# Batch 0 of a windowed attention feeding a gated two-matmul layer: scores four blocks wide, values read where they land, whole copies, weights loaded in smaller pieces, a new table of biases

## The chip, the cores and the metric

One core of one Trainium2 chip runs the kernel. The metric is the device time in microseconds (us) of one execution; the kernel before takes 299.81 us (median of 3 runs, 299.52 to 299.89). Engines are named as the profile names them: PE is TensorE (its weight loads are PEld), DVE is VectorE, ACT is ScalarE, POOL is GpSimd, SP is the sync engine, which only issues transfers.

## The reference

Attention over 8 batches, 8 heads, 576 rows and a head width of 64, followed by a layer with a sigmoid gate over all 4608 rows:

```python
scores = scale * np.matmul(q, k.transpose(0, 1, 3, 2))
rel = pos[:, None] - pos[None, :]
mask_plain = (rel >= 0) & (rel < 32)
mask_dil = (rel >= 0) & (rel < 32 * 4) & (rel % 4 == 0)
# heads 0-3 use mask_plain, heads 4-7 mask_dil; softmax over the unmasked scores
attn_out = np.matmul(attn, v)
x = attn_out.transpose(0, 2, 1, 3).reshape(4608, 512)
h = x @ w_in                      # 512 -> 2048
g = h * (1.0 / (1.0 + np.exp(-beta * h)))
out = g @ w_out                   # 2048 -> 512
```

So a row sees at most 32 keys: the 32 before it in the plain heads, every fourth of 128 in the dilated ones. Nearly all of the arithmetic is in the two matrix products.

## The kernel before, in words

**The layer.** The rows are cut into nine tiles of 512. For each tile t, `slot_h` runs 16 times (fb, 128 of the 2048 columns each): four matmuls of 512 columns (L901) of `w_in_bf` with `xT`, the transposed attention output; a tanh on ACT (L910); the gate on DVE (L915), which writes `g`. `block` runs four times per tile (128 rows each): 16 matmuls (L936) in four parts, each part with four fb of `w_out_bf` and needing only the quarter of w_out that it reads; then the result leaves PSUM through ACT or DVE (L951, L953) and is stored by SP. The first four fb of tile 0 are "apart": they first multiply the dilated half of x (kt 2, 3) and only then the plain half, in two pieces of rows.

**The attention**, `attention(b, ...)`, goes through a batch with named steps. x = 0, 1 are the two pairs of plain heads, x = 2, 3 the two pairs of dilated heads. In batches 0 to 2 q and k come from DRAM as rows (cast to bf16 on the way) and are transposed on PE (KD, QD for the dilated heads, L483; KP, QP for the plain ones, L493) and copied out of PSUM. S steps are scores. The plain rows are cut into six blocks of 96 queries per pair of heads; a plain score step of batches 0 and 1 takes three blocks (j = 0 or 1) of one x for both heads into two PSUM banks (L761), from batch 3 on all blocks go at once, four to a bank (L725). In batch 0 a mask is added in PSUM before the scores, as a matmul of the identity with a band of 0 and -65536 (L687, L747, L750); later batches multiply by a mask after the exponential (L637). The exponential is on ACT (L633). V steps are the products with v (L802 dilated, L818 plain): v carries a 65th column of ones, so that the last column is the softmax sum; DVE then takes its reciprocal and scales (L652, L653). X steps transpose the result back on PE (L855, L870) and copy it into `xT` (L862 and L878, through the helper at L257). T, U and Y do the same for the last 16 dilated positions of each residue.

The dilated v lands in `vd16` without the column of ones; the step `spread` (L619 to L625) copies it into `vd`, which has that column, in every batch. The dilated output of one x is copied into `xT` in two halves of time (L859): 288 and 224 columns.

**The order of the work** is worked out when the program is built. Each step is an operation in class `Plan` with the engines it can run on, an assumed cost, its dependencies and a due value `vt`. The plan picks, again and again, the operation that can start first by its model, and among those that start about equally early on an engine the one with the smallest `vt`. `NUDGE` adds a bias of so many ns to the start of the operation with a given number before the comparison (76 of about 1300 operations have one; the numbers count the operations as they are made, so that any operation added or left out shifts those behind it). `CAPS` says how many PSUM banks, of eight, each kind of step may hold at once: "o" is for output blocks, 3 of them. Each engine then executes its own list strictly in that order. Where PE would have nothing to do before 80 us the plan inserts a filler, a matmul on zeros (L1057, L1059). At most eight transfers per issuing engine are outstanding; the next issue waits for the oldest.

**Loads.** POOL issues the casting loads. In order of due value: batch 0's q, k and v (-9 to -8.4); w_in in three pieces of 512, 512 and 1024 columns (-7.3 to -7.28, L967); batch 1's q and k rows (-7.25 to -7.22) with w_out's first half between them (-7.235), batch 1's dilated v (-7.20), w_out's second half (-7.19, L972), batch 1's plain v (-7.19). POOL also builds the masks, as operations of its own: the tail mask (due -7.295), `mask_d` (-7.215) and `mask_n` (-7.183).

## Time and profile before

| | before |
|---|---|
| time, median of 3 runs (lowest, highest) | 299.81 us (299.52, 299.89) |
| the profiled execution: span, first to last instruction | 298.3 us |
| mean granted TensorE clock | 0.999 |
| first h matmul (L901) | 18.44 us |
| first output matmul (L936) | 34.81 us |
| first h matmul of tile 1 | 52.09 us |
| last PE work ends | 295.2 us |
| DMA, mean over the span | 141 GB/s |

The profile shows one execution. Its span is 298.3 us; the time of a run also holds what lies before the first and after the last instruction, and the median of the runs is 1.5 us above that span. A timeline row gives the start, the length, the engine and line, the operation with output and inputs, how many instructions are merged, and in brackets how long the engine idled before it and what ended that. PE's matmuls are pipelined: the length of a row includes the last one's latency, so rows overlap. A group row gives the busy time of the group, the mean ns of one instruction, and the idle time before them with its releasers. A row of the chain has a start, a length and what worked. Sizes of loads are those at the destination, in bf16.

### The profile page before, as it was taken

What the parts mean: (1) busy time and instruction counts of PE and PEld (TensorE: products, weight loads), DVE (VectorE), ACT (ScalarE), POOL (GpSimd) and SP (SyncE); (2) the same over time, 40 slices, a digit from 0 to 9 for tenths busy, and PEclk for the clock granted to TensorE, in tenths of its full rate; (3) what the DMA queues carried; (4) which work ended last, traced back from release to release, by engine and by line L of the source; (5) the groups of instructions that cost most, each with busy time, mean ns of one, the idle gap of its engine ahead of it and who ended that gap; (6) DMA issues with size and microseconds to landing.
All of it is one profiled execution on the core that took longest, in us unless ns stands there. A gap on an engine that the chain in (4) does not pass through costs nothing.

```text
span 298.3 us, 6224 instructions
## 1 busy us (share of the span) xinstructions
PE 293.0 (98%) x2424; PEld 149.8 (50%) x2424; DVE 186.1 (62%) x422; ACT 169.8 (57%) x308; POOL 90.4 (30%) x126
## 2 busy tenths in 40 slices
PE   8999999999999999999999999999999999999995
PEld 6765456545554445444544454445444444444454
DVE  4879668888767658774589358936891075433300
ACT  3768876867456738642487348634862376445311
POOL 8987354654283026600551065000100000000000
PEclk9999999999999999999999999999999999999999
DMA  7999999999979995999999989995115200010122
GB/s 150 187 208 202 206 196 210 154 163 184 185 124 226 151 199 124 171 136 240 184 188 155 200 174 196 162 186 147 38 31 124 73 0 36 35 37 37 63 76 73
DMA packets 111249, 42.00 MB, mean 141 GB/s; under 512 B 87620, under 2 KB 104596, under 8 KB 111220
## 3 DMA queue, kind: packets, MB, share of 16 engines
q0 software_dynamic: 60336, 18.58, 59.6%
q1 hardware_dynamic: 50740, 22.95, 36.4%
q8 instruction: 19, 0.31, 0.4%
q10 hardware_dynamic: 144, 0.07, 0.1%
q14 instruction: 10, 0.08, 0.1%
HBM read 37.76 MB, written 18.87 MB: 190 GB/s over the span
## 4 chain that ended last, share of the span: by engine, by line
PE 86%; DMA 8%; POOL 2%; DVE 1%; issue 1%; ACT 0%; POOLq 0%
PE bank L936 42%; PE bank L901 36%; DMA w_out_bf<-in_moe_w_out_dram 6%; DMA w_in_bf<-in_moe_w_in_dram 2%; PE bank L818 2%; PE bank L697 1%; PE bank L802 1%; PE bank L725 1%; POOL vp L408 1%; PE bank L787 1%; PE bank L666 0%; PE bank L761 0%; POOL st L408 0%; DVE g L915 0%; PE bank L493 0%
## 5 line engine op out<-in xcount | busy, mean ns | idle before, releaser
L936 PE MATMUL bank<-w_out_bf,g 128*128 128x512 bf16 (+2 forms) x608 | 136.6, 368 | 0.4 <-DMA w_out_bf<-in_moe_w_out_dram 0.4
L901 PE MATMUL bank<-xT,w_in_bf 128*128 128x512 bf16 (+2 forms) x584 | 134.8, 376 | 0.1
L915 DVE SCALAR_TENSOR_TENSOR g<-tnh,bank 128x512 bf16<-128x512 bf16 x144 | 96.5, 683 | 51.5 <-ACT tnh L910 50.3
L910 ACT ACTIVATE tnh<-bank,beta_half 128x512 bf16<-128x512 f32 x144 | 98.4, 690 | 53.2 <-PE bank L901 47.4
L901 PEld LDWEIGHTS <-w_in_bf 128*128 128x128 bf16 x584 | 55.1, 98 | 60.6 <-issue 0.2
L936 PEld LDWEIGHTS <-g 128*128 128x128 bf16 x608 | 55.2, 98 | 57.8 <-DMA w_out_bf<-in_moe_w_out_dram 0.5
L951 ACT ACTIVATE osb<-bank 128x512 f32<-128x512 f32 (+1 forms) x30 | 17.6, 592 | 34.1 <-PE bank L936 29.5
L633 ACT ACTIVATE ptd<-bank 128x512 bf16<-128x512 f32 x32 | 17.0, 600 | 21.4 <-PE bank L697 21.4
L633 ACT ACTIVATE pt<-bank 128x384 bf16<-128x384 f32 (+1 forms) x54 | 21.1, 463 | 6.5 <-PE bank L725 4.1
L637 DVE TENSOR_TENSOR pt<-pt,mask_n 128x384 bf16<-128x384 bf16 (+1 forms) x39 | 14.5, 378 | 12.1 <-ACT pt L633 11.6
L653 DVE TENSOR_TENSOR xsp<-bank,rcp 96x384 bf16<-96x384 f32 x32 | 17.7, 554 | 1.1
L637 DVE TENSOR_TENSOR ptd<-ptd,mask_d 128x512 bf16<-128x512 bf16 x25 | 10.9, 448 | 11.3 <-ACT ptd L633 10.4
L953 DVE TENSOR_SCALAR osb<-bank 128x512 f32<-128x512 f32 (+2 forms) x8 | 4.9, 607 | 20.5 <-PE bank L936 20.5
L652 DVE RECIPROCAL rcp<-bank 128x4 f32<-128x4 f32 (+2 forms) x72 | 12.8, 177 | 3.5 <-PE bank L818 1.4
L408 POOL DMA_DIRECT2D vt<-in_v_dram x16 | 13.7, 864 | 4.0 <-DMA w_out_bf<-in_moe_w_out_dram 2.9
L637 POOL TENSOR_TENSOR pt<-pt,mask_n 128x288 bf16<-128x288 bf16 (+1 forms) x7 | 5.3, 764 | 31.2 <-ACT pt L633 31.2
L653 DVE TENSOR_TENSOR xdm<-bank,rcp 128x256 bf16<-128x256 f32 x32 | 13.6, 424 | 1.1
L408 POOL DMA_DIRECT2D s<-in_k_dram x10 | 12.9, 1286 | 0.6 <-issue 0.6
L1015 POOL COPY pace<-xT 1x2 bf16<-1x2 bf16 x4 | 0.7, 176 | 39.2 <-DMA xT<-x 39.2
L408 POOL DMA_DIRECT2D s<-in_q_dram x10 | 12.2, 1220 | 0.1
L818 PEld LDWEIGHTS <-pt 128*128 128x128 bf16 x192 | 8.9, 97 | 4.4
L408 POOL DMA_DIRECT2D vp<-in_v_dram x9 | 10.2, 1129 | 1.0 <-DVE g L915 0.8
(113 smaller groups left out, 186.8 us busy)
## 6 DMA issues: line engine op xcount, KB each, us to landing
out_dram<-osb SPq DMA_DIRECT2D x35, 256.0 KB, 3.8
s<-in_q_dram POOLq DMA_DIRECT2D x10, 288.0 KB, 10.2
s<-in_k_dram POOLq DMA_DIRECT2D x10, 288.0 KB, 9.0
w_out_bf<-in_moe_w_out_dram POOLq DMA_DIRECT2D x2, 1024.0 KB, 17.4
vp<-in_v_dram POOLq DMA_DIRECT2D x7, 288.0 KB, 13.5
st<-in_q_dram POOLq DMA_DIRECT2D x6, 288.0 KB, 10.0
x<-xsp SPq DMA_DIRECT2D x12, 144.0 KB
st<-in_k_dram POOLq DMA_DIRECT2D x5, 288.0 KB, 13.2
```

The source lines that it names most:

```text
L408: {"POOL": nc.gpsimd, "SP": nc.sync}[queue].dma_start(out=out, in_=in_)
L633: nc.scalar.activation(out=w(), in_=sc(), func=ACT.Exp, scale=SCALE)
L637: E[e].tensor_tensor(out=w(), in0=w(), in1=m(), op=ALU.mult)
L652: nc.vector.reciprocal(out=r, in_=p[..., D])
L653: nc.vector.tensor_tensor(out=dst, in0=p[..., 0:D], in1=r.unsqueeze(len(p.shape) - 1).to_broadcast(list(p.shape[:-1]) + [D]), op=ALU.mult)
L818: nc.tensor.matmul(pv[:, a, h2, :], lhsT=lhs, rhs=vp[kv][:, (2 * x + h2) * NI + 3 * j + a, 0:D + 1], start=True, stop=True)
L901: nc.tensor.matmul(bank(g)[:, a:z], lhsT=w_in_bf[:, kt, fb * P:(fb + 1) * P], rhs=xT[:, kt, xo + a:xo + z], start=(i == 0 and kt == kts[0] ...
L910: nc.scalar.activation(out=th[:, 0:n], in_=bank(g)[:, 0:n], func=ACT.Tanh, scale=beta_half[:, fb:fb + 1])
L915: nc.vector.scalar_tensor_tensor(out=g_t[t % 2][:, fb, c0:c0 + n], in0=th[:, 0:n], scalar=1.0, in1=bank(g)[:, 0:n], op0=ALU.add, op1=ALU.mult)
L936: nc.tensor.matmul(bank(g)[:, lo:hi], lhsT=g_t[t % 2][:, fb, tb * P:(tb + 1) * P], rhs=w_out_bf[:, fb, lo:hi], start=(fb == 0), stop=(fb = ...
L951: nc.scalar.mul(out=ob[:, lo:hi], in_=bank(g)[:, lo:hi], mul=0.5)
L953: nc.vector.tensor_single_scalar(out=ob[:, lo:hi], in_=bank(g)[:, lo:hi], scalar=0.5, op=ALU.mult)
```

## The change

All of it but the biases and the bank count touches batch 0 and the loads of the weights.

- **Plain scores, batch 0** (`FOURS`): three steps of four blocks in the place of four steps of three blocks. The twelve blocks of the two x run through, so that the second step holds blocks 4, 5 of x = 0 and 0, 1 of x = 1. Six exponentials of 384 columns stand in the place of eight of 288, and the values of x, j wait for the steps that hold their blocks. The mask matmuls and their columns stay. The dependencies at batch 1 are extended, since batch 0 now lays its blocks out otherwise in the same buffer.
- **Dilated values, batch 0** (`LANDED`): no `spread`. The product reads `vd16` directly, 64 columns wide, and a second matmul of one column, with the ones of `vd[0]`, gives the sum: 16 matmuls more. The reader recorded for `vd16` is then the value step and not the copy.
- **Dilated copies, batch 0** (`WHOLE`): one copy of 512 columns per x into `xT` in the place of two.
- **Weights**: w_in in five pieces (256, 256, 512, 512, 512 columns; due -7.30 to -7.26), w_out in four (due -7.257, -7.256, -7.182, -7.181), each part of an output block waiting for its own quarter.
- **Order**: `CAPS["o"]` 4; `NUDGE` is a new table of some 760 entries between -2500 and 2500 ns.

```diff
-    CAPS = {"h": 4, "p": 4, "o": 3, "z": 4, "a": 8, "s": 5, "w": 6}
+    CAPS = {"h": 4, "p": 4, "o": 4, "z": 4, "a": 8, "s": 5, "w": 6}
-    NUDGE = {6: 2500, 32: -2500, 44: 150, 45: -400, 58: -150, 72: 60, 76: -400, 88: -400, 96: 60,
...
+    NUDGE = {0: -150, 1: -60, 2: -2500, 3: -900, 4: -150, 5: -60, 6: 150, 7: -60, 8: -60, 9: -60,
...
+    LANDED = 1
+    WHOLE = 1
+    FOURS = 1
...
-        o = plan.op([("POOL", 1100), ("DVE", 620), ("ACT", 1030)], spread,
-                    [ld["vd"][0], (fill3, fill4)[kv]] + war(("vd", kv)), vt, sbuf=True)
...
+        if b >= LANDED:
+            o = plan.op([("POOL", 1100), ("DVE", 620), ("ACT", 1030)], spread, ...
+            vdeps["D"] = [o]
+        else:
+            vdeps["D"] = [ld["vd"][0], fill3]
...
+            if b < FOURS:
+                if x and j:
+                    continue
+                m = 2 * j + x
+                blocks = range(4 * m, 4 * m + 4)
...
+                before = plan.op([("PE", 2 * mm(4 * QT) + 50)], added, [ident, adds["P"]], vt, acquire=gs)
+                sop = plan.op([("PE", 4 * mm(QT))], score,
+                              [o for y in sorted({n // NI for n in blocks}) for o in steps[f"KP{y}"] + steps[f"QP{y}"]] + [before],
+                              vt, group=gs, halves=True)
...
+                            src, n = (vd[kv], D + 1) if b >= LANDED else (vd16, D)
+                            nc.tensor.matmul(pv[:, r, a, 0:n], lhsT=ptd[:, x - 2, j, 2 * r + a],
+                                             rhs=src[:, 2 * (x - 2) + a, 2 * r + j, 0:n],
                                              start=True, stop=True)
+                            if b < LANDED:
+                                nc.tensor.matmul(pv[:, r, a, D:D + 1], lhsT=ptd[:, x - 2, j, 2 * r + a],
+                                                 rhs=vd[0][:, 0, 0, D:D + 1], start=True, stop=True)
...
-                for j, (t0, t1) in enumerate(((0, CT // 2), (CT // 2, P))):
+                for j, (t0, t1) in enumerate(((0, P),) if b < WHOLE else ((0, CT // 2), (CT // 2, P))):
...
-    for n, (c0, c1) in enumerate(((0, 512), (512, 1024), (1024, 2048))):
+    for n, (c0, c1) in enumerate(((0, 256), (256, 512), (512, 1024), (1024, 1536), (1536, 2048))):
...
-    for n in range(2):
-        o = load("POOL", (w_out_bf[:, 8 * n:8 * n + 8, :],
-                          moe_w_out[n * 8 * P:(n + 1) * 8 * P, :].rearrange("(c p) d -> p c d", p=P)),
-                 [], (-7.235, -7.19)[n], 2048, .41)
-        w_out_ld[2 * n] = w_out_ld[2 * n + 1] = o
+    for n in range(4):
+        w_out_ld[n] = load("POOL", (w_out_bf[:, 4 * n:4 * n + 4, :],
+                                    moe_w_out[n * 4 * P:(n + 1) * 4 * P, :].rearrange("(c p) d -> p c d", p=P)),
+                           [], (-7.257, -7.256, -7.182, -7.181)[n], 1024, .41)
```

## The prediction

> **What bounds the kernel now.** I read the page's busy table first.

> ```profile
> PE 293.0 (98%) x2424; PEld 149.8 (50%) x2424; DVE 186.1 (62%) x422; ACT 169.8 (57%) x308; POOL 90.4 (30%) x126
> ```

> TensorE (PE) is busy for 293.0 of 298.3 us, so the only time to be had is time in which it does nothing of use. The windows, cut at the first h matmul, the first w_out matmul and the first matmul of tile 1, show where that is (columns: window, its length, busy us of PE, PEld, DVE, ACT and POOL with instruction counts, granted clock, DMA share, GB/s).

> ```profile
> 10.00:18.44 8.44, 8.11 (x193) 6.17 (x188) 7.90 (x23) 6.08 (x17) 7.33 (x12) 1.00 1.52 193
> 18.44:34.81 16.37, 15.98 (x128) 8.73 (x119) 12.42 (x26) 13.53 (x23) 10.57 (x18) 1.00 1.24 206
> 34.81:52.09 17.28, 17.28 (x245) 9.51 (x246) 12.38 (x34) 12.38 (x31) 8.84 (x11) 1.00 1.53 203
> 100.00:200.00 100.00, 99.89 (x708) 48.49 (x708) 69.01 (x154) 56.26 (x100) 30.66 (x35) 1.00 1.38 178
> ```

> From 18.44 on PE idles 0.39 us up to 34.81, nothing in the next window and 0.11 in the hundred that stand for the middle. Before 18.44 its busy time deceives: the PE timeline (start, length, what, count, idle before it) shows fillers, matmuls on zeros that the plan puts wherever PE would wait.

> ```profile
> 11.22 0.71 PE L1059 MATMUL bank<-zero 128*128 128x256 bf16 x5
> 12.10 0.39 PE L1059 MATMUL bank<-zero 128*128 128x256 bf16 x2
> 12.57 0.41 PE L802 MATMUL bank<-vd,ptd 128*128 128x65 bf16 x8
> 12.82 0.38 PE L1059 MATMUL bank<-zero 128*128 128x256 bf16 x2
> 15.52 0.82 PE L1059 MATMUL bank<-zero 128*128 128x256 bf16 x6
> 17.22 0.38 PE L1059 MATMUL bank<-zero 128*128 128x256 bf16 x2
> 18.03 0.48 PE L493 MATMUL bank<-ident_b,st 64*64 64x64 bf16 x36 [0.25 <-DMA st<-in_q_dram]
> 18.44 1.04 PE L901 MATMUL bank<-xT,w_in_bf 128*128 128x512 bf16 x4
> 34.81 1.04 PE L936 MATMUL bank<-w_out_bf,g 128*128 128x512 bf16 x4 [0.39 <-DMA w_out_bf<-in_moe_w_out_dram]
> ```

> Six fillers take 0.82 us and two 0.38, so one more costs 0.44 / 4 = 0.11 us. From 11.22 to 18.44 there are 5+2+2+6+2 = 17, or 1.9 us. With the waits of 0.25 and 0.39 that makes 2.5 us; this is all the front has to give after 11 us. The engine that holds PE up there is VectorE: 7.90 busy of 8.44.

> **Values where they land, whole copies, wider scores.** The DVE timeline of batch 0:

> ```profile
> 11.26 0.75 DVE L257 COPY qT<-bank 128x576 bf16<-128x576 bf16 x1
> 12.03 0.43 DVE L257 COPY vd<-vd 128x1024 bf16<-128x1024 bf16 x1
> 12.69 0.42 DVE L257 COPY vp<-vp 32x640 bf16<-32x640 bf16 x1 [0.23 <-DMA vp<-in_v_dram]
> 13.04 0.16 DVE L652 RECIPROCAL rcp<-bank 128x4 f32<-128x4 f32 x1
> 17.02 0.76 DVE L257 COPY xT<-bank 128x288 bf16<-128x288 bf16 x2
> 19.08 0.28 DVE L637 TENSOR_TENSOR ptt<-ptt,mask_t 96x256 bf16<-96x256 bf16 x1
> 33.08 0.84 DVE L637 TENSOR_TENSOR ptd<-ptd,mask_d 128x512 bf16<-128x512 bf16 x2
> ```

> The removed spread is the vd copy at 12.03. The first dilated values (12.57) come right behind it, and the first norm at 13.04 behind those. Without it the values wait for the load and for their exponentials:

> ```profile
> 5.33 1.00 POOL L408 DMA_DIRECT2D vd<-in_v_dram  x1
> vd<-in_v_dram POOLq DMA_DIRECT2D x1, 256.0 KB, 6.4
> 9.48 1.57 ACT L633 ACTIVATE ptd<-bank 128x512 bf16<-128x512 f32 x3
> ```

> The load lands at 5.33 + 6.4 = 11.7 (the last column of such a row is us from issue to landing), and three of the four exponentials end by 9.48 + 1.57 = 11.05. So the values can run at 11.8 and the norm can start at 11.8 + 0.4 = 12.2, once DVE has finished qT at 12.01. That is up to 0.8 earlier. Each group now also issues a one-column matmul beside each of its four, 16 in all. PE runs eight 65-column ones in 0.24 us further on, 0.03 each:

> ```profile
> 44.63 0.24 PE bank L802 x8
> 40.91 0.23 PE bank L761 x6
> 41.15 0.97 PE bank L936 x4
> 42.90 1.73 PE bank L936 x8
> ```

> So the sixteen cost at most 0.48 us of PE and more than nothing, because they are issued one by one. I take the upper end, the same kind of matmul; what hides them is the 1.9 us of fillers, and if those were gone the 0.48 would be paid. On the chain, eight of them stand ahead of the first norm at worst: 0.2 us. I take 0.6 for the spread, with ends 0 (DVE then only waits for something else, the halo of vp at 12.69 being the next late thing) and 0.8. [...]

> The whole dilated copy replaces 288 + 224 columns by 512. By groups, ScalarE takes 403 and 359 ns for the two, and VectorE 403 and 380:

> ```profile
> L257 ACT COPY xT<-bank 128x288 bf16<-128x288 bf16 x9 | 3.5, 403 | 1.1 <-PE bank L870 1.0
> L257 ACT COPY xT<-bank 128x224 bf16<-128x224 bf16 x3 | 1.1, 359 | 0.0
> L633 ACT ACTIVATE pt<-bank 128x384 bf16<-128x384 f32 x30 | 12.6, 501 | 4.1 <-PE bank L725 4.1
> L633 ACT ACTIVATE pt<-bank 128x288 bf16<-128x288 f32 x24 | 8.5, 415 | 2.4 <-PE bank L761 2.2
> ```

> A slope of 44 ns per 64 columns puts the whole one at 403 + 154 = 557 on ACT, 0.2 less than two, but if two engines would have shared the halves it is 0.15 later than the longer of them. Before, X3's two copies ran one behind the other on DVE (17.02, 0.76), and the first h matmul waits for them, so I take a gain of 0.1 (from -0.15 to +0.2). Six exponentials of 384 instead of eight of 288 are 6 x 501 = 3.0 against 8 x 415 = 3.3 us of ACT. ACT has 2.4 us free in that window, so I take 0 (0 to 0.3). Mask matmuls and scores keep their columns, 8 x 288 = 6 x 384 = 2304, and cost nothing new. The values of x = 1 now wait for the third score group, but their output is read last: the four "apart" groups start on the dilated rows, 8 matmuls at 1.73 / 8 = 0.22, 1.7 us of cover. Without it that wait is late next.

> **The first h matmul.** At 18.03 PE stands 0.25 us in front of the second batch's q transposes, which are not needed yet. With loads and biases reordered I expect those behind the first h: they are moved, not saved, so only the 0.25 counts (0 if another wait takes the place).

> **Weights.** Loads from POOL land in the order issued:

> ```profile
> 9.58 6.91 DMA w_in_bf<-in_moe_w_in_dram
> 16.78 0.91 POOL L408 DMA_DIRECT2D w_out_bf<-in_moe_w_out_dram  x1 [0.44 <-DMA w_in_bf<-in_moe_w_in_dram]
> 12.20 1.51 POOL L408 DMA_DIRECT2D w_in_bf<-in_moe_w_in_dram  x2
> w_in_bf<-in_moe_w_in_dram POOLq DMA_DIRECT2D x1, 512.0 KB, 8.3
> w_in_bf<-in_moe_w_in_dram POOLq DMA_DIRECT2D x1, 1024.0 KB, 12.5
> 25.71 0.90 POOL L408 DMA_DIRECT2D w_out_bf<-in_moe_w_out_dram  x1 [0.66 <-DMA w_in_bf<-in_moe_w_in_dram]
> w_out_bf<-in_moe_w_out_dram POOLq DMA_DIRECT2D x1, 1024.0 KB, 16.7
> st<-in_q_dram POOLq DMA_DIRECT2D x1, 288.0 KB, 6.5
> ```

> w_in's three pieces land at 9.58 + 6.91 = 16.5, 12.20 + 8.3 = 20.5 and about 12.95 + 12.5 = 25.4 (the two issues at 12.20 share 1.51), w_out's halves at about 34.8, when PE's wait ends, and 25.71 + 16.7 = 42.4. So the 1024 KB of the third piece took 4.9 us, 209 KB per us. Of w_out's first half the first quarter is enough to begin: behind the same bytes it lands 512 / 209 = 2.4 us before 34.8, at 32.3, and ahead of the second rows earlier still. The wait of 0.39 goes; with h begun about 1 us sooner PE gets there at 33.4, and the quarter is there. w_in's first piece, halved, lands 256 / 209 = 1.2 sooner, at 15.3, ahead of any h I expect. Two issues are added for each matrix, at 0.75 to 0.9 us of POOL each, 3.4 in all. Behind them on POOL stand the tail mask, first read at 19.08, and the masks of batch 1, first read at 33.08; all were built by 25, so the second have 8 us of cover. The tail mask has less, and its reader delays only batch 0's tail rows, which the first h tile doesn't read. The issue at 16.78 stood behind the landing of an earlier one, so smaller pieces free it sooner, too.

> What a cut costs in the queue the rows bound: between 16.5 and 20.5 landed the second rows' q of 288 KB and w_in's second piece of 512, 800 KB in two loads in 4.0 us, where 209 KB per us makes 3.83. So a further load costs at most 0.17 us and perhaps nothing; w_in's two would put w_out's first quarter at 32.6, still ahead of PE. [...]

> **A fourth o bank and new biases.** The critical rows above show the price of going from 64-row matmuls back to whole ones: four dense ones in 0.97 after L761, 0.86 otherwise, 0.11 per return. There are as many score groups after batch 0 as before, so I take 0 for the order (from -0.5 to +0.5: about five returns won or lost). The fourth bank lets four output blocks, not three, run on the first half of w_out: 1.73 us more work before 42.4.

> **The sum**: 0.6 + 0.1 + 0.25 + 0.39 = 1.3 us. The profiled span is 298.3, the median of the runs 299.81, so 1.5 lies around the span and is unchanged: span 297.0, time **298.5 us**.

> **Rivals.**
> *All of the front goes.* If every filler from 11.22 on is replaced by work, 2.5 less the 0.48 of one-column matmuls is 2.0, with order up to 0.5: 297.3 to 297.8. For it: DVE is that window's only full engine and all parts relieve it or ACT. Against it: eight norms still have to pass DVE.
> *Nothing comes through.* The first h may still wait: for vp's second half, for q rows, or since a bias of up to 2500 ns overrules a due time and leaves a load where it was, so that the change does not do what it says. Then the spread's 0.43 only becomes another wait: 299.4 to 300.
> *The weights run into the second rows.* Total bytes up to 42.4 don't shrink. PE, 1 us early, has 16 x 0.86 = 13.8 of h(0), then 4 x 2 x 0.86 = 6.9 of output on the first half, and some 4 to 5 us of batch 1 (an estimate: the third window's 17.28 less thirteen sets of w_out matmuls at 0.86 leaves 6.1 for batch work in all of it). From 17.4 that lasts to about 42.5. If the third quarter falls behind two more row loads (2 x 288 KB, 2.8 us), it lands at about 42.4 - 2.4 + 2.8 + 1.4 (vp's 288) = 44.2, PE stands 1.7, and batch 1, whose scores then come late too, adds about as much again: 298.5 + 3.4 = 301.9. It decides once that quarter lands after 42.5. Against it: due times put it behind vp alone, 41.4.
> *The pieces cost queue time.* With 0.17 for each, four delay the last quarter by 0.7, from about 42.4 to 43.1, after the third at 40.7; PE has the third's 3.5 us of output in between, so it would stay at 298.5. Only from 0.8 / 2 = 0.4 us per piece on does the first quarter come behind PE's 33.4 (32.3 plus two pieces), and each further 0.1 is worth 0.2. At 1 us a piece: 299.7, and slower from about 1.4 on. [...]

> **How the numbers follow.** Forecast 0.50, all of the front 0.17, nothing 0.18, weights in the way 0.13, pieces at over a us 0.02. A change under 0.2%, 0.6 us, can't be told from none: faster means below 299.2, slower above 300.4. So faster 0.67; same 0.19, with half of the pieces; slower 0.14. The range leaves out the last two and little more: 297.1 to 300.2.

> **What would show it.** Right: no vd copy on DVE before 13, first norm at about 12.4, fewer than ten fillers between 11 and the first h, that first h near 17.4 with no L493 wait ahead of it, no PE wait before the first w_out matmul, and the window from it to tile 1 still full. Wrong: a first h at 18 or later, PE waits on w_out or w_in landings between 25 and 50, fillers after 20, or more dense groups at 0.97.

## The result, and the profile after

The changed kernel takes 303.77 us (median of 4 runs, 303.56 to 304.41) against 299.85 (4 runs, 299.52 to 300.14) for the kernel before beside it: a ratio of 1.0126, 95% interval 1.0106 to 1.0145. That is 3.9 us slower, where 1.3 us faster had been forecast. Four of the runs below have one execution in a slower state, at least 1.5% above the fastest of the same kernel; medians and ratios leave it out. The profiled execution has a span of 302.1 us (298.3 before). Its page begins:

```profile
span 302.1 us, 6167 instructions
PE 291.3 (96%) x2394; PEld 150.1 (50%) x2433; DVE 186.9 (62%) x414; ACT 171.2 (57%) x306; POOL 96.5 (32%) x135
```

39 of the 2433 matmuls have no record here (PE counts 2394, its weight loads 2433), so a gap of 0.1 or 0.2 us on PE in this trace need not be one. The windows, cut as in the prediction at the first h matmul, the first output matmul and tile 1's first (columns as there):

```profile
17.46:32.91 15.45, 15.12 (x112) 8.37 (x115) 11.83 (x24) 11.31 (x21) 10.97 (x17) 1.00 1.27 205
32.91:54.60 21.69, 20.90 (x322) 11.84 (x324) 17.61 (x46) 15.67 (x37) 11.31 (x16) 1.00 1.52 203
100.00:200.00 100.00, 98.39 (x677) 47.99 (x689) 65.77 (x143) 57.51 (x101) 33.58 (x39) 1.00 1.27 166
```

The first h matmul comes at 17.46, as forecast, and the first output matmul 1.9 us sooner than before. Tile 1 comes 2.5 us later. I added up the useful matmul work still to come at 22.5 us in both traces, by weight loads and their usual spacing: the changed kernel is 1.05 us behind there, and loses 1.0 more by its last matmul, which ends at 297.2 instead of 295.2. The remaining 1.8 us of the span lies behind the last matmul (4.9 us from there to the end, 3.1 before). Three places, then.

**The end.** The last rows on the timeline, first of the kernel before, then of the changed one (ACTq is ACT's instruction queue, here issuing the last store):

```profile
295.03 0.28 ACT L951 ACTIVATE osb<-bank 128x128 f32<-128x128 f32 x1 [1.40 <-PE bank L936]
295.59 0.37 ACTq L956 DMA_DIRECT2D out_dram<-osb  x1
```

```profile
297.57 0.28 ACT L1094 ACTIVATE osb<-bank 128x128 f32<-128x128 f32 x1 [1.06 <-PE bank L1079]
297.60 2.16 ACTq L1099 DMA_DIRECT2D out_dram<-osb  x1
```

The same issue takes 2.16 us instead of 0.37: the 1.8 us. The transfers of the changed kernel between 298 and 299 us hold one packet of a kind that the last 3 us of the kernel before do not have (queue and kind: packets, MB, share):

```profile
q14 instruction: 1, 0.01, 2.9%
```

It is an instruction transfer of 8 KB, inside the 2.16 us. In all traces of this case the last such packet comes after 445 to 449 records of ACT. Before, that was at 250.9 us, and nothing waited. ACT's records include the semaphore events on which it waits, and the new order needs 143 of them instead of 196. So the border between two such packets, which lay at 250.9 us, now seems to lie on the kernel's last store; the first experiment tests this.

**The front.** PE's timeline of the changed kernel:

```profile
4.58 2.80 PE L1201 MATMUL bank<-zero 128*128 128x256 bf16 x16
7.21 0.68 PE L574 MATMUL bank<-ident_b,st 96*128 96x96 bf16 x12
17.46 0.59 PE L1044 MATMUL bank<-xT,w_in_bf 128*128 128x512 bf16 x2
18.25 0.38 PE L1044 MATMUL bank<-xT,w_in_bf 128*128 128x512 bf16 x1
19.18 1.02 PE L1044 MATMUL bank<-xT,w_in_bf 128*128 128x512 bf16 x4
20.17 0.38 PE L1201 MATMUL bank<-zero 128*128 128x256 bf16 x2
20.80 1.53 PE L1044 MATMUL bank<-xT,w_in_bf 128*128 128x288 bf16 x12
32.91 1.03 PE L1079 MATMUL bank<-w_out_bf,g 128*128 128x512 bf16 x4
```

No q transposes of the second batch stand directly ahead of the first h, and no wait directly ahead of the first output matmul at 32.91. But the first h is early in name only: eight matmuls (one has no record) in 3.3 us, between transposes, products with v and two fillers, and a dense run from 20.80. What it waits for is on ACT and DVE, where the last rows of batch 0 are made:

```profile
17.47 0.87 ACT L727 ACTIVATE pt<-bank 128x384 bf16<-128x384 f32 x2
18.45 0.40 ACT L348 COPY xT<-bank 128x288 bf16<-128x288 bf16 x1
```

```profile
13.45 0.17 DVE L746 RECIPROCAL rcp<-bank 128x4 f32<-128x4 f32 x1
16.27 0.68 DVE L348 COPY xT<-bank 128x512 bf16<-128x512 bf16 x1
17.50 0.55 DVE L747 TENSOR_TENSOR xsp<-bank,rcp 96x384 bf16<-96x384 f32 x1
20.05 0.55 DVE L747 TENSOR_TENSOR xsp<-bank,rcp 96x384 bf16<-96x384 f32 x1
21.00 0.31 DVE L348 COPY xT<-bank 128x288 bf16<-128x288 bf16 x1 [0.40 <-PE bank L1013]
```

The third score group's exponentials end at 18.34, the last norm at 20.60, the last copy to xT at 21.31. The spread is gone from DVE as forecast; the first norm is later than before all the same (13.45 against 13.04). The key transposes came at 7.21 instead of 6.35, behind sixteen fillers instead of nine, and from them to the first norm it is 6.24 us instead of 6.69. How much of the 0.86 is the order's can't be read from one execution: the fillers run at two speeds (sixteen in 1.92 or 3.08 us, below, under the zero fill). Why is the first h early, then? Before, the first two norms of plain heads stood on DVE ahead of the second pair's dilated copies to xT at 17.02; this is the first of the two:

```profile
15.78 0.55 DVE L653 TENSOR_TENSOR xsp<-bank,rcp 96x384 bf16<-96x384 f32 x1
```

Now the dilated copy goes first (16.27) and the plain norms follow (17.50). The new order gave the first h its time at the expense of the plain rows, which the same tile needs next.

**The middle.** Its one large stall is at 156 us (PE, then DVE and POOL, of the changed kernel):

```profile
156.43 2.75 PE L1044 MATMUL bank<-xT,w_in_bf 128*128 128x512 bf16 x12 [0.60 <-DVE g L1058]
```

```profile
152.94 2.84 DVE L731 TENSOR_TENSOR pt<-pt,mask_n 128x384 bf16<-128x384 bf16 x2
152.48 1.98 POOL L731 TENSOR_TENSOR pt<-pt,mask_n 128x384 bf16<-128x384 bf16 x1
153.34 2.22 POOL L348 COPY vd<-st 128x1024 bf16<-128x1024 bf16 x1
```

Two masks that take 0.36 us each elsewhere took 2.84 on DVE while POOL ran a mask and a copy; the gate behind them came late.

### The profile page after: what moved, and what is told of

It reads as the page before. It is cut to its first block, busy times and chain, and to the rows that moved or that the text cites. A ratio compares the mean times of both kernels' runs of the same rounds, so it can differ in the third digit from the quotient of the medians.

```text
span 302.1 us, 6167 instructions
## 1 busy us (share of the span) xinstructions
PE 291.3 (96%) x2394; PEld 150.1 (50%) x2433; DVE 186.9 (62%) x414; ACT 171.2 (57%) x306; POOL 96.5 (32%) x135
## 3 DMA queue, kind: packets, MB, share of 16 engines
q1 hardware_dynamic: 50740, 22.95, 34.8%
## 4 chain that ended last, share of the span: by engine, by line
PE 92%; DVE 4%; issue 1%; ACT 0%; ACTq 0%; DVEq 0%
PE bank L1079 40%; PE bank L1044 39%; PE bank L961 2%; PE bank L939 2%; PE bank L791 2%; DVE pt L731 1%; PE bank L1201 1%; PE bank L574 1%; PE bank L860 1%; PE bank L1199 1%; PE bank L584 1%; DVE xsp L747 1%; PE bank L923 1%; PE bank L896 0%; DVE g L1058 0%
## 5 line engine op out<-in xcount | busy, mean ns | idle before, releaser
L1053 ACT ACTIVATE tnh<-bank,beta_half 128x512 bf16<-128x512 f32 x144 | 96.5, 687 | 70.3 <-PE bank L1044 58.1
L1044 PE MATMUL bank<-xT,w_in_bf 128*128 128x512 bf16 (+1 forms) x567 | 133.8, 376 | 1.4 <-DVE g L1058 0.6
L1044 PEld LDWEIGHTS <-w_in_bf 128*128 128x128 bf16 x584 | 55.1, 98 | 61.0 <-issue 0.9
L1094 ACT ACTIVATE osb<-bank 128x512 f32<-128x512 f32 (+2 forms) x32 | 18.7, 585 | 26.5 <-PE bank L1079 26.2
L727 ACT ACTIVATE pt<-bank 128x384 bf16<-128x384 f32 (+1 forms) x52 | 20.8, 472 | 6.1 <-PE bank L860 3.2
L731 DVE TENSOR_TENSOR pt<-pt,mask_n 128x384 bf16<-128x384 bf16 (+1 forms) x39 | 15.9, 425 | 6.9 <-ACT pt L727 6.6
L731 DVE TENSOR_TENSOR ptd<-ptd,mask_d 128x512 bf16<-128x512 bf16 x24 | 10.0, 422 | 8.6 <-ACT ptd L727 8.0
L731 POOL TENSOR_TENSOR ptd<-ptd,mask_d 128x512 bf16<-128x512 bf16 x4 | 4.6, 1152 | 32.9 <-ACT ptd L727 27.0
L499 POOL DMA_DIRECT2D vt<-in_v_dram x16 | 14.7, 921 | 1.4 <-DMA w_out_bf<-in_moe_w_out_dram 1.4
L499 POOL DMA_DIRECT2D s<-in_k_dram x10 | 12.2, 1224 | 0.3 <-issue 0.3
L731 POOL TENSOR_TENSOR pt<-pt,mask_n 128x384 bf16<-128x384 bf16 (+1 forms) x7 | 6.8, 986 | 16.0 <-ACT pt L727 13.1
L961 PE MATMUL bank<-vp,pt 128*128 128x65 bf16 x192 | 10.6, 193 | 0.1
## 6 DMA issues: line engine op xcount, KB each, us to landing
out_dram<-osb SPq DMA_DIRECT2D x35, 256.0 KB
s<-in_k_dram POOLq DMA_DIRECT2D x10, 288.0 KB, 10.5
s<-in_q_dram POOLq DMA_DIRECT2D x10, 288.0 KB, 8.4
w_out_bf<-in_moe_w_out_dram POOLq DMA_DIRECT2D x4, 512.0 KB, 12.9
vp<-in_v_dram POOLq DMA_DIRECT2D x7, 288.0 KB, 11.0
st<-in_q_dram POOLq DMA_DIRECT2D x6, 288.0 KB, 10.2
w_in_bf<-in_moe_w_in_dram POOLq DMA_DIRECT2D x3, 512.0 KB, 9.5
```

The source lines that it names most:

```text
L499: {"POOL": nc.gpsimd, "SP": nc.sync}[queue].dma_start(out=out, in_=in_)
L727: nc.scalar.activation(out=w(), in_=sc(), func=ACT.Exp, scale=SCALE)
L731: E[e].tensor_tensor(out=w(), in0=w(), in1=m(), op=ALU.mult)
L961: nc.tensor.matmul(pv[:, a, h2, :], lhsT=lhs, rhs=vp[kv][:, (2 * x + h2) * NI + 3 * j + a, 0:D + 1], start=True, stop=True)
L1044: nc.tensor.matmul(bank(g)[:, a:z], lhsT=w_in_bf[:, kt, fb * P:(fb + 1) * P], rhs=xT[:, kt, xo + a:xo + z], start=(i == 0 and kt == kts[0] ...
L1053: nc.scalar.activation(out=th[:, 0:n], in_=bank(g)[:, 0:n], func=ACT.Tanh, scale=beta_half[:, fb:fb + 1])
```

## The experiments

Where a kernel is said to have an order written out, the plan's choices are replaced by a fixed list of operations with their engines and banks; with the list of the kernel it was taken from it is that kernel again, instruction for instruction. All ratios are against the kernel before on the same chip, with 95% intervals.

**Small exponentials on ACT at the start of the changed kernel**, to move the border in ACT's instructions and nothing else.

```diff
         nc.scalar.activation(out=warm[:], in_=warm[:], func=ACT.Exp)
+        for _ in range(10):
+            nc.scalar.activation(out=spare[:], in_=warm[:], func=ACT.Exp)
```

> The changed kernel with ten small exponentials more on ScalarE, behind its first one, where it idles from 2.3 to 5.1 us; nothing else. Theory A (ScalarE fetches its instructions in blocks, and in the changed kernel the border of a block falls on its very last store, whose issue then takes 2.16 us instead of 0.37): the border moves ten instructions forward, into a time when ScalarE waits anyway, the last issue takes about 0.4 again and the time is 302.0 us, 1.8 below the changed kernel. Theory B (the long issue is the store waiting for the two stores that SyncE issues beside it): nothing moves, 303.8.

301.45 us, ratio 1.0055 (1.0031 to 1.0078). The tail:

```profile
296.76 0.28 ACT L1097 ACTIVATE osb<-bank 128x128 f32<-128x128 f32 x1 [0.78 <-PE bank L1082]
296.87 0.37 ACTq L1102 DMA_DIRECT2D out_dram<-osb  x1
```

The issue is back at 0.37 us and the last packet on the instruction queue comes at 285 us. Ten small instructions added at the start take 2.1 us off by the ratios. That the store waited for SP's two stores beside it, the other theory, is ruled out: those are still there. It holds over the whole study: the four kernels in the new order whose last packet comes at 297 or 298 us (the changed one, the zero fill first, w_in's piece moved, the masks off POOL) issue the last store in 2.16 to 2.22 us, have 4.9 to 5.0 us behind the last matmul and take 303.11 to 303.90 us. The four in which it comes at 285 or 286 issue it in 0.37, have 3.1 behind the last matmul and take 300.88 to 301.60. So the profiles put 1.8 us on the store itself; the rest of the 2.1 lies within the spread of the runs.

**Zero fill first**, so that PE starts early, in the changed kernel's written-out order.

```diff
-3:V: 13:S: 0:V: 16:G: ...
+0:V: 3:V: 13:S: 16:G: ...
```

> The changed kernel's order kept as it is, but VectorE's zero fill put first again, so that the first filler matmuls can start at 1.1 instead of 1.55 us. Theory A (the late start let PE's clock rise at 6.4 instead of 4.0 us, and nine 256-column fillers at 0.213 us instead of 0.109 then held up the first key transposes): the clock rises near 4 us, the first key transposes start at 6.3 instead of 7.2, and up to 0.9 us comes back if nothing else is late: 303.0. As the plain values are late by their loads too, 303.4 is as likely. Theory B (the clock's rise has nothing to do with the start of the fillers): it rises at 6.4 again and the time stays at 303.8.

What is called the clock's rise here was read from the spacing of the fillers: in the changed kernel the first nine of the sixteen take 0.19 to 0.21 us each, up to 6.45, and the others 0.11; in the kernel before all nine take 0.11 to 0.12, from 4.09 on. The granted clock reads 1.00 in both, so that the clock makes the difference was not shown.

303.11 us, ratio 1.0105 (1.0080 to 1.0129): under the changed kernel's 1.0126, but the intervals overlap. PE begins at 1.14 us instead of 1.55, and the keys come no sooner:

```profile
1.14 3.09 PE L1083 MATMUL bank<-zero 64*64 64x64 bf16 x108 [1.14 <-DVE warm L291]
4.16 3.08 PE L1085 MATMUL bank<-zero 128*128 128x256 bf16 x16
7.08 0.68 PE L458 MATMUL bank<-ident_b,st 96*128 96x96 bf16 x12
```

Sixteen fillers took 3.08 us, not 16 x 0.11 = 1.8. In the kernel with the masks off POOL, whose start is that of the changed kernel, the same sixteen took 1.92:

```profile
4.57 1.92 PE L1085 MATMUL bank<-zero 128*128 128x256 bf16 x16
6.33 0.68 PE L458 MATMUL bank<-ident_b,st 96*128 96x96 bf16 x12
```

So the late start does not fix when the keys come; in the kernels of this study that have the new front with all sixteen fillers it lies between 6.33 and 7.53.

**w_in's second piece behind the plain loads of v**, in the changed kernel's order (there it is issued ahead of them, at 5.68 us).

```diff
-36:G: f0 27:G: ... 22:G: ... 24:G: ... 26:G: ... 28:G:
+36:G: f0 ... 22:G: ... 24:G: ... 26:G: 27:G: ... 28:G:
```

> The changed kernel's order kept as it is, but the second piece of w_in, which POOL there issues at 5.7 us ahead of both plain value loads, is issued behind the first piece. Theory A (that piece made the plain values of batch 0 late, so that PE starts the first h tile at 17.5 and then stands or fills until 20.8): the plain values land 1.3 us earlier, the dense h work begins about 1 us earlier, 302.8 to 303.2. Theory B (the plain rows are late because the third score group of four blocks comes last): the loads land earlier, the dense h work still begins at 20.8, 303.8.

303.47 us, ratio 1.0114 (1.0096 to 1.0133): 0.3 us by the medians, not told from nothing. The loads of v are issued 0.8 us sooner (6.56 against 7.35), but PE now waits 0.60 us for the piece of w_in, and the dense run begins at 20.59 against 20.80.

**Only the smaller pieces of the weights**, in the old order: the kernel before with w_in in five and w_out in four loads at the places of its three and two.

> The kernel before in its own order, with only the weights cut into the five and four pieces of the change, each piece issued where its parent was. Theory A (the pieces cost nothing and the loss is all in the new order): the wait of 0.39 us before the first w_out matmul goes, 299.4 to 299.9. Theory B (the pieces pay a fixed time each in the queue, or their issues hold up POOL): w_out comes later than before, PE waits for it, 301 or more.

300.04 us, ratio 0.9996 (0.9982 to 1.0011). By themselves the pieces neither cost nor bring anything that can be measured. The wait for w_out is gone, but this profile doesn't show what the pieces would have gained there: its front was late (first h at 19.36, after a wait of 0.64 for q rows at 8.24), so that PE came to w_out only at 35.39.

**Values where they land and whole copies in the old order** (`FOURS = 0`, the spread and two half copies left out of the old list).

> Before's own order of all operations, written out as a fixed list, with two of the change's parts put in at the places that their operations have there: in the first batch the values are used where they land (no spread copy, sixteen one-column multiplications more), and each dilated tile goes to xT in one whole copy. Wide scores, weights and biases stay as before. Theory O (the parts are sound, the new order lost the time): the copy of 0.6 us is gone from VectorE, the chain to the first h may be up to 0.6 us earlier, and the time is 299.3 (298.9 to 299.9), with the end of the profile as before's (last store's issue near 0.4 us). Rival P (the parts themselves cost: one whole copy holds its engine longer and the extra one-column multiplications delay the values): 300.4 or more, with the first h later than 18.4 us.

299.85 us, ratio 0.9989 (0.9980 to 0.9998): 0.3 us faster. This is the one kernel of the study whose interval lies below the kernel before, and by less than the 0.7 forecast for these two parts. DVE's rows:

```profile
13.37 0.53 DVE L232 COPY vp<-vp 32x640 bf16<-32x640 bf16 x1 [0.36 <-DMA vp<-in_v_dram]
14.05 0.18 DVE L630 RECIPROCAL rcp<-bank 128x4 f32<-128x4 f32 x1 [0.15 <-PE bank L827]
```

The spread is gone, and DVE waits 0.36 us for the halo of vp and 0.15 for PE in its place: from the keys to the first norm it is 6.68 us, as before (6.69). This is the lower end that the forecast gave the spread, 0.

**All parts of batch 0 in the old order** (`FOURS = 1`, the fourth score group's places left out, tile 0's values ahead of tile 1's).

> As the run with the landed values and whole copies in before's order, and the first batch's plain scores in three pairs of four blocks instead of four pairs of three, at the places of the first three pairs; the fourth pair's places are left out, and the values of tile 0 come ahead of those of tile 1 as in the changed kernel. Weights as before. Theory O: two exponentials fewer and the parts' copies gone, so that the first h comes at 17.4 to 18.1 us and the time is 299.0 (298.5 to 299.7). Rival P: the values of tile 1 wait for the last pair's exponentials behind everything else, h starts at 18.5 us or later and the time is 300.3 or more.

300.17 us, ratio 1.0002 (0.9992 to 1.0013). The wide scores bring nothing that can be measured, and the rival that the parts of batch 0 themselves cost falls too: with the old order they are within 0.13% of the kernel before, where the changed kernel is 1.26% above. The first h stood at 19.04 here, later than the 17.4 to 18.1 expected, and the time is that of the kernel before.

**Masks off POOL**: in the changed kernel's order its 13 masks on POOL stand on DVE (V for G in the list; the first four shown).

```diff
-252:G: ... 250:G: ... 417:G: ... 535:G: ...
+252:V: ... 250:V: ... 417:V: ... 535:V: ...
```

> The changed kernel with its order kept; the 13 masks that it gives to GpSimd are on VectorE instead, at the same places in the list. Theory M (VectorE's two masks at 152.94 us took 2.84 us instead of 0.72 because GpSimd ran a mask and a copy beside them, and the gate queued behind them stopped TensorE for 0.60 us): the two masks take 0.36 us each, the stall before L1044 near 156 us is gone, and the time is 303.1 (302.7 to 303.5). Rival (the two masks wait for something else, or VectorE's added 13 x 0.36 us push gates back): 303.7 or more.

303.90 us, ratio 1.0125 (1.0100 to 1.0149): no change. The profile did what it should, though. DVE, then PE:

```profile
152.17 1.74 DVE L615 TENSOR_TENSOR pt<-pt,mask_n 128x384 bf16<-128x384 bf16 x2
```

```profile
154.91 2.75 PE L928 MATMUL bank<-xT,w_in_bf 128*128 128x512 bf16 x12
```

The masks take 1.74 us (a copy still runs on POOL beside them), and the h matmuls no longer wait. By the same count of work to come, 0.12 us is lost between 150 and 160 us instead of 0.88 in the changed kernel, but 1.35 instead of 0.68 between 160 and 220: what the stall had cost was spent later. Part of that is a new wait, for a mask that had moved to DVE:

```profile
215.94 0.33 PE L845 MATMUL bank<-vp,pt 128*128 128x65 bf16 x5 [0.32 <-DVE pt L615]
```

So the stall is real, and moving all thirteen masks is worth nothing that can be measured; what the stall alone costs, this run doesn't show, since it takes 0.60 away and puts 0.32 elsewhere.

**Three mends at once** on the changed kernel: ten small exponentials, w_in's second piece behind v, 7 fillers fewer ahead of the keys. The kernel also had the masks on DVE, as the one above, which its expectation does not name.

> The changed kernel with its order kept but for three things at once: ten small exponentials more on ScalarE at the start, w_in's second piece behind the values' plain loads, and 7 of the 16 wide filler multiplications ahead of the first key transposes left out. If the losses add up (2.1 for the late issue of the last store, 0.3 for the piece of w_in, 0.5 to 0.9 for the fillers that ran past the keys' arrival): 300.7 (300.2 to 301.3). If the front's parts hide each other (the first half of the keys is late anyway, or the clock rises later with fewer fillers): 301.4 or more.

301.60 us, ratio 1.0050 (1.0036 to 1.0063): no better than the small exponentials alone. PE's rows show what was lost again:

```profile
6.12 0.68 PE L461 MATMUL bank<-ident_b,st 96*128 96x96 bf16 x12 [0.21 <-ACT st L232]
17.50 0.60 PE L931 MATMUL bank<-xT,w_in_bf 128*128 128x512 bf16 x2 [1.04 <-DMA w_in_bf<-in_moe_w_in_dram]
```

The keys came 1.1 us sooner, and the first h waited 1.04 us for the piece of w_in that I had moved back. One mend undid the other, and the masks on DVE brought their wait of 0.32 us along, here at 216.93.

**A square of orders.** Four kernels of the same operations (all the change's parts, ten small exponentials), with the order cut at the first tanh and each half from one of the two lists (where the PSUM bank that a list names is still held, another one is taken). First the old front with the new rest:

> One corner of a square of four kernels with the same operations (all of the change's parts, and ten small exponentials more at the start of ScalarE, so that its last store is issued without the 2.16 us). The order is cut just ahead of the first tanh (about 21 us): here the front has the old order, all behind it the new one. Of the 1.6 us that the new order lost apart from the last store, the profile of the changed kernel shows about 1.0 by 22.5 us and about 1.0 behind that. If each half of the order carries its own loss: 300.9 (300.5 to 301.3), and the corner with the halves exchanged gives the same. Rival (the loss of the front is hidden by the old rest, so that the new rest carries all of it): 301.5 or more, with the exchanged corner within 0.3 of the all-old one.

304.92 us, ratio 1.0141 (1.0102 to 1.0180). The new front with the old rest:

> The corner with the new order up to the first tanh and the old one behind it; same operations and ScalarE's ten small exponentials as the other three. If each half carries its own loss: 300.9 (300.5 to 301.3). Rival (the old rest waits for its own later parts anyway and hides a late front): within 0.3 of the all-old corner, 299.9 to 300.3.

313.13 us, ratio 1.0435 (1.0422 to 1.0449). Both old:

> The corner with the old order throughout, all of the change's parts in it (the weights' smaller pieces too) and ScalarE's ten small exponentials. Expected as the run of all parts in the old order, 300.1 (299.8 to 300.5); 300.8 or more would say that the pieces and the parts together cost what each alone did not.

300.45 us, ratio 1.0025 (1.0009 to 1.0040). Both new:

> The corner with the new order throughout: the changed kernel with ScalarE's ten small exponentials again, beside the other three. 301.7 (301.2 to 302.1); the difference from the all-old corner, 1.6, is what the order costs apart from the last store.

301.58 us, ratio 1.0049 (1.0034 to 1.0064). Neither theory of the halves holds: each mixture is worse than both pure corners, so the loss doesn't belong to a half. In the first, PE's longest wait was for a transposed row transfer:

```profile
114.82 1.90 PE L949 MATMUL bank<-xT,w_in_bf 128*128 128x512 bf16 x8 [3.13 <-DMA xT<-x]
```

In the second it waited for the second batch's q rows (PE, then POOL's issues of those rows; then the same issues in the all-old corner):

```profile
33.17 0.70 PE L489 MATMUL bank<-ident_b,st 64*64 64x64 bf16 x36 [10.87 <-DMA st<-in_q_dram]
```

```profile
20.45 0.71 POOL L404 DMA_DIRECT2D st<-in_q_dram  x1
22.26 0.64 POOL L404 DMA_DIRECT2D st<-in_q_dram  x1 [1.10 <-DMA w_in_bf<-in_moe_w_in_dram]
```

```profile
12.01 0.71 POOL L404 DMA_DIRECT2D st<-in_q_dram  x1
17.76 0.65 POOL L404 DMA_DIRECT2D st<-in_q_dram  x1 [0.81 <-DMA w_in_bf<-in_moe_w_in_dram]
```

The new front issues the weights first and the rows 8.4 and 4.5 us later, which the new rest is arranged for: it transposes them later. PE, which takes its work in order, stood 10.87 us in front of transposes that the old rest had put early. This is the forecast's rival of weights and second rows the other way round, with the rows behind the weights, in a kernel made by hand; the changed kernel itself has no wait of this kind. The all-old corner also gives what the order costs apart from the last store: 301.58 less 300.45, 1.1 us by medians (0.0049 less 0.0025, 0.7, by ratios, whose intervals leave 0.1 to 1.4). The all-old corner is itself 0.25% above the kernel before, and its interval doesn't reach 1: all parts, the pieces and the ten exponentials together cost some 0.7 us there, and no run tells which of them does.

**The fillers alone**: seven of the sixteen left out of the new order (with the small exponentials), and seven added to the kernel before.

> The changed kernel with ten small exponentials more on ScalarE at the start (its last store is then not late) and 7 of the 16 wide filler multiplications ahead of the first key transposes left out; w_in's second piece stays ahead of the values' plain loads, so that the first h does not wait for it. Theory F (the fillers that ran past the keys' arrival are what the new order's front lost): key transposes near 6.2 us, the first h near 16.5 us, and 300.7 (300.3 to 301.2), 0.9 under the same kernel with all its fillers (301.6). Rival (the rest of the new order waits elsewhere for what the front gained): 301.3 or more although the first h is early.

300.88 us, ratio 1.0031 (1.0009 to 1.0053): by the ratios 0.5 us under the same kernel with all its fillers, though the intervals overlap (1.0049, 1.0034 to 1.0064). Its keys came at 6.32, no sooner than behind all sixteen fillers in the kernel with the masks off POOL (6.33).

> The kernel before with 7 more wide filler multiplications ahead of its first work on TensorE, sixteen as in the changed kernel, and nothing else. Theory F: the first key transposes come up to 1 us later while the clock is low, all of the front behind them too, and the time is 300.8 (300.4 to 301.2). Rival (what comes behind the front waits for DMA anyway, so that a late front is hidden): 300.1 to 300.3, with the first h late.

299.97 us, ratio 1.0006 (0.9995 to 1.0018). Its front is late and its end is not:

```profile
4.08 1.92 PE L1031 MATMUL bank<-zero 128*128 128x256 bf16 x16
6.71 0.68 PE L455 MATMUL bank<-ident_b,st 96*128 96x96 bf16 x12
19.29 1.04 PE L873 MATMUL bank<-xT,w_in_bf 128*128 128x512 bf16 x4
295.60 0.37 ACTq L928 DMA_DIRECT2D out_dram<-osb  x1
```

The first h is 0.85 us later than in the kernel before (18.44): 0.36 from the keys, and PE's waits for q rows came to 0.73 (0.15 and 0.58) instead of 0.25. The last store is issued 0.01 later (295.59). Its PE has no wait for w_out, where the kernel before stands 0.39 us; so 0.39 of the 0.85 is hidden there, and where the rest goes these rows don't show. In the old order a late front is hidden; a rule of my sum was that it is not. In the new order the fillers may cost half a us; that is not settled.

## Why the prediction was wrong, by its own steps

**"I take 0 for the order (from -0.5 to +0.5)" is the step that failed.** It priced the order by the returns from 64-row matmuls to whole ones alone (0.11 us each, by the rows of before). Those did not change: by the weight loads, of which no record is missing, there are 22 behind 22 us in the kernel before and 22 in the changed one. The order cost 3.0 to 3.7 us all the same, the changed kernel's 1.0126 against 1.0025 and 1.0002 for the parts in the old order with and without the pieces and the exponentials. Of this, 1.8 went through the last store by the profiles (2.1 to 2.3 by the ratios of three kernels with ACT's instructions shifted, 1.0055, 1.0050 and 1.0049), and 0.7 to 1.6 lies in how operations and loads lie to one another (0.7 between the two pure corners; 1.6 between the small exponentials' kernel and all parts in the old order, 1.0055 and 1.0002). The intervals are too wide for the two to add up to the last tenth. The profile of before could not have shown the first part, but the sum held it tacitly: "1.5 lies around the span and is unchanged" was right (303.82 less 302.1 in the profiled execution is 1.7), and the 3.1 us from the last matmul to the end of the span was never a term, so that nothing asked what it consists of.

**The sum's premise, that the front passes to the end one for one, failed as well.** 0.6 for the spread and 0.1 for the whole copy: measured together 0.3 (0.06 to 0.6) in the old order, and nothing of it by the first norm, where DVE waited for the halo of vp and for PE. The 0.39 for w_out: with smaller pieces the wait is gone, and 300.04 against 300.06 is what that was worth; it goes, too, when PE is merely late (the added fillers). A wait for a transfer behind the front would be the other side of an early front, taking whatever the front gains up to it; the runs show only the mirror of this, a front 0.85 us late at no cost. I had named that case, "Nothing comes through", with 0.18; for the old order it is close to what the runs show. The 0 for the wide scores was near (1.0002 against 0.9989, with intervals that overlap).

**"The first h near 17.4" was right (17.46), by luck, and told nothing.** The forecast had it follow from a first norm at 12.4, and that came at 13.45; what made the first h early was the order, which put the plain norms behind the dilated copy and the second batch's q transposes (0.41 us and their wait of 0.25) behind the first h. The step that carried it over to the work behind was "1.7 us of cover" for the values of x = 1, "without it that wait is late next". It was: the third group's exponentials ended at 18.34, the values and norms of x = 1 at 20.60, the last copy at 21.31, some 3.8 us behind the first h, where I had given 1.7. The test that I had set, the first h's time, should have been the start of the dense run: 20.80, against 20.01 before.

**Right in the particulars:** no vd copy on DVE; none of the second batch's q transposes directly ahead of the first h; no wait for w_out; the pieces of the weights free by themselves, so the range for a further load (0 to 0.17 us) held at its lower end. Nine loads of 256 to 512 KB in the place of five of 512 to 1024 KB (sizes at the destination) gave a ratio of 0.9996. **Wrong in the particulars:** the first norm at 13.45 instead of 12.4, eleven fillers between 11 us and the first h, where fewer than ten were forecast, and three after 20, which I had called a sign of being wrong; the fillers ahead of the keys, seven more of them, had no term at all (2.80 / 16 = 0.175 us each, not the 0.11 read further on); and the window from the first output matmul to tile 1, which was to stay full and shows 0.79 us idle, an unknown part of it the missing records.

What stays open: which of the new order's differences make up the 0.7 to 1.6 us. The sixteen fillers may be 0.5 of it. The stall at 156 us may be as much: in the all-new corner, whose trace lacks no matmul, PE idles 0.51 us between 22 and 290 us, all of it there, in the all-old corner 0.06, and the run that removed the stall made another. The halves can't be told apart by exchanging them.

## What to carry to other kernels

Where a change comes with a new order, price the order first and try the parts in the old order: in the old order the parts here came out between 0.3 us faster (two of them) and 0.7 slower (all, with ten small exponentials), and the new order cost 3.0 to 3.7. Read the last 5 us of a profile as a chain of its own, issue by issue, because nothing behind it can hide a stall there. And look at what stands between an early gain and the end: here a front that was 0.85 us late cost nothing in the old order, so a front that is early need not bring anything either.

## What the hardware showed that I had not expected

```profile
4.15 2.10 PE L1086 MATMUL bank<-zero 128*128 128x256 bf16 x9
7.37 0.68 PE L458 MATMUL bank<-ident_b,st 96*128 96x96 bf16 x12
```

  Nine took 2.10 us here and 1.16 in the kernel before, and the keys came at 7.37 instead of 6.35, though this kernel's median is the lower one. The granted clock reads 1.00 in both. A change of the first 7 us can't be read from one profile. What sets the speed, no run here shows.
- Masks on DVE beside a mask and a copy on POOL took 1.42 us each instead of 0.36, and 0.87 each beside the copy alone. The copy took 2.22 us on POOL in the first case, 1.71 in the second and 1.04 in the kernel before, at 155.99. Why both engines are slower together, no run here shows.
